# Storing the body's outputs through ScalarE's DMA queue instead of SyncE's, in a fused attention and token-mixing kernel

## The chip, the cores and the metric

The kernel runs on one core of one Trainium2 chip. A core has five engines that run their own instruction streams in order: TensorE (PE; its weight loads are listed apart as PEld), VectorE (DVE), ScalarE (ACT), GpSimd (POOL) and SyncE (SP). An engine's stream may also hold DMA issues: the engine waits for what the transfer needs, hands the transfer over, and goes on. SP computes nothing; its stream here is a queue of DMA issues. The metric is the device time of one execution in microseconds; less is better.

## The reference

Eight batches of 3200 rows go through a gated attention with squared ReLU, and its result through a token-mixing layer:

```python
# attention, per batch: z is 3200x64, u and v are 3200x256
scores = (1/S) * z @ z.T
attn   = maximum(scores, 0) ** 2
x      = u * (attn @ v)
# mixing, per batch
wq, wk = x @ w_q, x @ w_k              # 3200x64 each
W_tok  = (1/8) * wq @ wk.T             # 3200x3200
out    = maximum(W_tok @ x, 0) @ w_out # 3200x256
```

The inputs and the output are float32. The kernel never forms `W_tok`: it computes `wk.T @ x` (64x256, called the heads) and multiplies `wq` by that.

## The kernel before

**Tiling.** The 3200 rows of a batch are 25 tiles of 128. For the output they are taken in 7 groups: six of 512 rows and a last one of 128 (`LASTG`). For each group the program makes the scores of the group against all 25 tiles, squares their ReLU into 16-bit tiles `at`, and multiplies those by `v` in two PSUM accumulators (L289). The scores matrix is symmetric, so a part of the `at` tiles is not computed a second time but turned by a DMA transpose on SP into `tt` and `ttl` (L268) and used in a later group.

**Phases.** The loop from L602 goes through phases k. A phase issues, in this order: six scores matmuls (L211), or four if it also mixes; the ReLU of these on DVE (L234) or ACT (L230); the squares of the scores of the phase before, on POOL (L249) or ACT (L247), with one of ACT's squares sometimes kept back; then the matmuls of the second product (L289), which read `at` tiles of two phases before and turned tiles. After the first ten of these matmuls one extra piece of work may be put in (`extra`, L681 to L701), and behind it stands the square that was kept back (L702). The order of each engine's stream is the order of the program's text.

**What follows a group.** When a group's accumulators are complete, DVE multiplies them by `u` (L315), SP transposes the result to `xT` (L327), and some phases later `keys_and_heads` (L528) makes the projections to queries and keys (L337), ACT copies them (`qk`, L348), SP transposes them to `kx` (L353), POOL doubles a half of `kx` (L362), and TensorE adds the group's share of the heads (L368). When a whole batch's heads are there, its groups are mixed one by one: `mix` (L416), a ReLU on ACT (`rt`, L428), and, as the `extra` of the same phase, `proj` (L441) and `proj_out`, which scales the result by a constant into `fo` and stores it. In the body `proj_out` gets one way: the scaling on ACT (L468), and the store of up to 512 KB on SP (L469). The last group of a batch, with 128 rows, goes a way of its own inside `keys_and_heads`: `side_proj_out` scales on ACT into `fs` (L509) and stores 128 KB on SP (L510). `fo` has two buffers and `fs` one.

**SP's queue.** In the body SP issues, in program order: the loads of `u` (L146), the transposes of `z` (L138), `at` (L268), `xT` (L327) and `kx` (L353), a copy of half of the queries to other partitions (L361), and the stores (L469, L510). An issue that waits holds all those behind it. POOL issues the loads of `v` and `z`.

**Tail.** After the loop (from L716) what is left of the last two batches is mixed and stored by `store`, with queues of its own: SP, and for one store of 256 KB ACT (L751). This is the only DMA that ACT issues.

Of the kernel before, what the change touches and what calls it, by code (L numbers as in the profile page):

```python
# [16 lines left out]
def kernel(  # L17
# [10 lines left out]
    nc = tc.nc  # L28
# [4 lines left out]
    P = 128  # L33
    NT = S // P
    ND = D // P
    W = 512
    widths = [512] * 6 + [128]
# [32 lines left out]
    def ps_tile(name):  # L70
        return pps.tile([P, 2, W], FP32, tag="ps", name=name)
# [9 lines left out]
    def rows(t, b):  # L81
        return t[b].rearrange("(p n) d -> p n d", n=NT)
# [122 lines left out]
    def scores(p0):  # L205
        pair = tiles[p0 : p0 + 2]
        sc = ps_tile("sc")
        for h, (b, gi, ti) in enumerate(pair):
            gs, gw = starts[gi], widths[gi]
            half = h * dqk  # L210
            nc.tensor.matmul(  # L211
                out=sc[:, h, 0:gw],
                lhsT=zT[b][half : half + dqk, ts(ti, P)],
                rhs=zT[b][half : half + dqk, ds(gs, gw)],
                start=True,
                stop=True,
            )
        return sc
# [192 lines left out]
    def mix(b, gi):  # L411
        gw = widths[gi]
        ps = ps_tile("mx")
        for db in range(ND):
            half = db * dh
            nc.tensor.matmul(  # L416
                out=ps[:, db, 0:gw],
                lhsT=hss[b][half : half + dh, ds(db * P, P)],
                rhs=qks[b, gi][half : half + dh, 0:gw],
                start=True,  # L420
                stop=True,
            )
        return ps
# [6 lines left out]
    def proj(b, gi, banks=None):  # L430
        rt = rts.pop((b, gi))
        nj = widths[gi] // P
        ps = None
        if banks is None:
            ps = ps_tile("fo")
            banks = [ps[:, 0, :], ps[:, 1, :]]
        for jf in range(0, nj, 2):
            n = min(2, nj - jf)
            for dc in range(ND):
                for j in range(jf, jf + n):  # L440
                    nc.tensor.matmul(  # L441
                        out=banks[jf // 2][:, ds((j - jf) * D, D)],
                        lhsT=rt[:, dc, ts(j, P)],
                        rhs=wo[:, dc, :],
                        start=(dc == 0 and j == jf),
                        stop=(dc == ND - 1 and j == jf + n - 1),
                    )
        return banks if ps is None else ps[:].rearrange("p a w -> p (a w)")

    def proj_out(b, gi, src, ways):  # L450

        n0 = starts[gi] // P
        if groups:
            fo = pfo.tile([P, 2, W], FP32, tag="fo", name="fo")
        else:
            fo = pg.tile([P, 2, W], FP32, tag="g", name="fo")
        flat_out = fo[:].rearrange("p a w -> p (a w)")
        at = 0
        for on_dve, queue, n in ways:
            sl = slice(at * D, (at + n) * D)  # L460
            part = src[at // 2][:, 0 : n * D] if isinstance(src, list) else src[:, sl]
            if on_dve:
                nc.vector.tensor_scalar(  # L463
                    out=flat_out[:, sl], in0=part, scalar1=FINAL_SCALE, scalar2=None,
                    op0=AOP.mult,
                )
            else:
                nc.scalar.mul(out=flat_out[:, sl], in_=part, mul=FINAL_SCALE)  # L468
            queue.dma_start(  # L469
                out=rows(out, b)[:, n0 + at : n0 + at + n, :],  # L470
                in_=flat_out[:, sl].rearrange("p (n d) -> p n d", d=D),
            )
            at += n
# [33 lines left out]
    def side_proj_out(b, ps):  # L507
        fo = pfo.tile([P, D], FP32, tag="fs", name="fs", bufs=1)
        nc.scalar.mul(out=fo[:], in_=ps[:, 1, D : 2 * D], mul=FINAL_SCALE)  # L509
        nc.sync.dma_start(out=rows(out, b)[:, NT - 1, :], in_=fo[:])  # L510


    todo_mix, todo_between, at_phase, side = [], [], {}, []
# [72 lines left out]
    def mix_due(k):  # L586
        if len(groups) > NG:
            return todo_mix and k - mixed_at[0] >= 3
        older = todo_mix and todo_mix[0][0] < last - 1
        return (older or len(todo_mix) > 2) and k - mixed_at[0] >= 2 and not key_due(k)  # L590
# [11 lines left out]
    while groups:  # L602
        now[0] = k
        for fn in at_phase.pop(k, []):
            fn()
        n = 4 if k == 0 else 6
        mixing = None
        if mix_due(k):
            mb, mg = todo_mix.pop(0)
            mixed_at[0] = k  # L610
            mixing = (mb, mg, mix(mb, mg))
            n = 4
        n = min(n, NTILE - produced)
        fresh = []
        for p0 in range(produced, produced + n, 2):
            fresh.append((p0, scores(p0)))
        produced += n
        made_by.append(produced)
        keying = not mixing and key_due(k)
        if keying and keyed:  # L620
            for g_ in keyed[0][1]:
                double_keys_queries(keyed[0][0], g_)
        if mixing:
            mix_out(*mixing)
        staged = []
        act_pair = 0 if (gate_pending or k < 4) else 1
        for i, (p0, sc) in enumerate(fresh):
            on_act = i == act_pair and not mixing
            staged.append((p0, first_stage(p0, sc, on_act)))
        if k < 3:  # L630
            turn_first(k + 1)
        if k < 2:

            for i, (p0, g) in enumerate(staged):
                second_stage(p0, g, i != 1)
            staged = []
        if len(waiting) == 3:
            second_on_act = [False, True, k % 2 == 0]
        else:
            second_on_act = [False, True]  # L640
        seconds = [(p0, g, a) for (p0, g), a in zip(waiting, second_on_act)]
        acts = [x for x in seconds if x[2]]
        for x in seconds:
            if not x[2]:
                second_stage(*x)
        for x in acts[:1]:
            second_stage(*x)

        if k == 0:
            k += 1  # L650
            continue
        ready = made_by[k - (1 if k < 3 else LAG)]
        b, gi = groups[0]
        begins = left is None
        if begins:
            group_begun(k, b, gi)
            need = ends[b, gi]
            scored = tiles[consumed:need]
            left = [t for t in range(NT) if (b, gi, t) not in scored]
            m = 2 if need <= made_by[k - 1] else 3 if need <= produced else 4  # L660
            if m == 4 and need > produced + (4 if mix_due(k + 1) else 6):
                m = 5
            if gi == LASTG:
                m = 1 if need <= ready else 2
            sizes = [NT * (i + 1) // m - NT * i // m for i in range(m)]
            if k == 1:
                sizes = [2, 4, 4, 5, 5, 5]
        size = sizes.pop(0)
        closes = not sizes
        new = min(ready, ends[b, gi]) - consumed  # L670
        if not closes:
            new = min(new, size)
        rows_ = [t for _, _, t in tiles[consumed : consumed + new]]
        old = len(left) if closes else min(len(left), size - new)
        rows_ += left[:old]
        left = left[old:]
        consumed += new
        assert rows_ and (not closes or consumed == ends[b, gi]), (k, b, gi, sizes)
        gate_pending = False
        matmuls = second_product(b, gi, rows_, begins, closes)  # L680
        extra = None  # L681
        if mixing:
            mb, mg, _ = mixing

            def extra():
                proj_out(mb, mg, proj(mb, mg), [(False, nc.sync, widths[mg] // P)])
        elif keying:
            extra = todo_between.pop(0)[1]
        cut = 10 if extra else 0
        if closes and (b, gi) == (last, LASTG):  # L690
            assert not extra
            cut = 20

            def extra():
                last_gram(last, LASTG - 1, psg)

            psg = acc_tile(1, "xtx")
        for fn in matmuls[:cut]:
            fn()
        if extra:  # L700
            extra()  # L701
        for x in acts[1:]:  # L702
            second_stage(*x)
        for fn in matmuls[cut:]:
            fn()
        if closes:
            group_done(k, b, gi)
            gate_pending = True
            groups.pop(0)
            left = None  # L710
        waiting = staged
        k += 1
# [69 lines left out]
```

## Time and profile before

| | |
|---|---|
| time, median of 3 runs | 803.76 us (801.42 to 806.72) |
| time of the profiled execution | 803.47 us |
| its span, first to last instruction | 801.7 us |
| PE busy | 787.7 us (98%) |
| DVE, ACT, POOL busy | 493.5 us, 476.8 us, 481.6 us |
| SP's hardware queue, share of the 16 DMA engines' span | 76.7% |
| POOL's software queue, the same | 17.8% |
| stores in the body | 40 of `fo`, 7 of `fs` |

Busy time of ACT does not count the issuing of DMAs. A DMA issue on SP has a duration of its own (how long the issue took) and a time to landing (from the issue to the arrival of the last byte): for the stores of 512 KB the median landing is 4.3 us, for `kx` 3.6 us. The matmuls' recorded durations overlap (a matmul of 256 columns has 273 ns, and the next one starts about 109 ns after it), so PE is judged by gaps and waits and not by its busy share.

### The profile page before, as it was taken

What the parts mean: (1) busy time and instruction counts of PE and PEld (TensorE: products, weight loads), DVE (VectorE), ACT (ScalarE), POOL (GpSimd) and SP (SyncE); (2) the same over time, 40 slices, a digit from 0 to 9 for tenths busy, and PEclk for the clock granted to TensorE, in tenths of its full rate; (3) what the DMA queues carried; (4) which work ended last, traced back from release to release, by engine and by line L of the source; (5) the groups of instructions that cost most, each with busy time, mean ns of one, the idle gap of its engine ahead of it and who ended that gap; (6) DMA issues with size and microseconds to landing.
All of it is one profiled execution on the core that took longest, in us unless ns stands there. A gap on an engine that the chain in (4) does not pass through costs nothing.

```text
span 801.7 us, 16689 instructions
## 1 busy us (share of the span) xinstructions
PE 787.7 (98%) x6778; PEld 584.6 (73%) x6778; DVE 493.5 (62%) x514; ACT 476.8 (59%) x528; POOL 481.6 (60%) x350
## 2 busy tenths in 40 slices
PE   7999999999999999999999999999999999999996
PEld 4777777777777777777777777777777767777784
DVE  5766666665665566755667556765666655675535
ACT  6655556556665666655566566656665565586534
POOL 7966677565666557755575556764677646454520
PEclk9999999999999999999999999999999999999999
DMA  7999799997989969999899979999899997769725
GB/s 176 145 215 193 125 175 181 211 192 136 216 144 227 195 137 203 164 213 177 189 160 195 206 176 169 179 184 203 179 179 175 185 204 170 159 147 208 178 50 224
DMA packets 330877, 143.20 MB, mean 179 GB/s; under 512 B 307440, under 2 KB 313136, under 8 KB 330800
## 3 DMA queue, kind: packets, MB, share of 16 engines
q1 hardware_dynamic: 302528, 125.90, 76.7%
q0 software_dynamic: 28128, 15.98, 17.8%
q8 instruction: 53, 0.87, 0.5%
q10 hardware_dynamic: 144, 0.26, 0.1%
q14 instruction: 24, 0.20, 0.1%
HBM read 59.38 MB, written 26.21 MB: 107 GB/s over the span
## 4 chain that ended last, share of the span: by engine, by line
PE 96%; issue 1%; ACT 1%; DVE 1%; POOL 0%; DMA 0%; POOLq 0%; DVEq 0%
PE acc L289 69%; PE sc L211 14%; PE fo L441 5%; PE qk L368 3%; PE qk L337 3%; PE mx L416 2%; PE ztp L118 0%; DMA z<-in_z_dram 0%; ACT g L230 0%; DVE fo L463 0%; POOL at L249 0%; PE qk L499 0%; PE xtx L393 0%; DVE g L234 0%; PE hd L403 0%
## 5 line engine op out<-in xcount | busy, mean ns | idle before, releaser
L249 POOL TENSOR_TENSOR at<-g 128x1024 f16<-128x1024 f32 (+1 forms) x232 | 426.4, 1851 | 231.5 <-DVE g L234 147.4
L234 DVE TENSOR_SCALAR g<-sc 128x1024 f32<-128x1024 f32 (+1 forms) x341 | 389.6, 1185 | 187.8 <-PE sc L211 185.6
L289 PE MATMUL acc<-v_sb,at 128*128 128x256 f16 x3656 | 447.0, 273 | 0.0
L289 PEld LDWEIGHTS <-at 128*128 128x128 f16 x3656 | 344.7, 98 | 107.6 <-issue 64.9
L230 ACT ACTIVATE g<-sc 128x1024 f32<-128x1024 f32 x127 | 130.0, 1024 | 192.9 <-PE sc L211 192.8
L247 ACT ACTIVATE at<-g 128x1024 f16<-128x1024 f32 (+2 forms) x236 | 239.0, 1029 | 0.6 <-DVE g L234 0.6
L289 PE MATMUL acc<-v_sb,tt 128*128 128x256 f16 x1152 | 149.1, 273 | 0.0
L211 PE MATMUL sc<-zT 64*128 64x512 f16 x920 | 129.3, 381 | 1.4 <-ACT zT L122 0.9
L289 PEld LDWEIGHTS <-tt 128*128 128x128 f16 x1152 | 112.5, 98 | 12.9
L315 DVE TENSOR_TENSOR x_sb<-acc,u_sb 128x512 f16<-128x512 f32 (+1 forms) x104 | 69.4, 668 | 64.2 <-PE acc L289 62.8
L428 ACT ACTIVATE rt<-mx 128x1024 f16<-128x1024 f32 (+1 forms) x49 | 49.3, 1010 | 61.7 <-PE mx L416 60.1
L211 PEld LDWEIGHTS <-zT 64*128 64x128 f16 x920 | 34.9, 95 | 48.6 <-issue 26.9
L362 POOL COPY kx<-kx 128x256 f16<-128x256 f16 (+1 forms) x54 | 20.2, 380 | 61.9 <-DMA kx<-qk 59.9
L468 ACT ACTIVATE fo<-fo 128x1024 f32<-128x1024 f32 (+1 forms) x41 | 41.5, 1013 | 23.1 <-PE fo L441 21.2
L441 PE MATMUL fo<-wo,rt 128*128 128x256 f16 x386 | 49.9, 273 | 1.0 <-DVE fo L463 0.9
L348 ACT CAST qk<-qk 128x512 f16<-128x512 f32 (+1 forms) x54 | 28.7, 544 | 25.5 <-PE qk L368 14.5
L441 PEld LDWEIGHTS <-rt 128*128 128x128 f16 x386 | 37.3, 98 | 6.8 <-issue 1.4
L381 DVE TENSOR_TENSOR ha<-ha,qk 128x256 f32<-128x256 f32 x31 | 13.1, 421 | 32.8 <-ACT qk L348 32.8
L337 PE MATMUL qk<-xT_sb,wqk 128*128 128x512 f16 (+1 forms) x108 | 29.9, 358 | 0.0
L368 PE MATMUL qk<-x_sb,kx 128*128 128x256 f16 x191 | 28.4, 273 | 1.4 <-POOL kx L362 1.4
L368 PEld LDWEIGHTS <-kx 128*128 128x128 f16 x195 | 18.9, 98 | 13.7 <-POOL kx L362 2.1
L289 PE MATMUL acc<-v_sb,ttl 128*128 128x256 f16 x192 | 22.6, 273 | 0.0
(47 smaller groups left out, 148.9 us busy)
## 6 DMA issues: line engine op xcount, KB each, us to landing
u_sb<-in_u_dram SPq DMA_DIRECT2D x48, 512.0 KB, 4.7
out_dram<-fo SPq DMA_DIRECT2D x46, 512.0 KB, 4.3
v_sb<-in_v_dram POOLq DMA_DIRECT2D x35, 320.0 KB, 6.0
qk<-qk SPq DMA_DIRECT2D x47, 64.0 KB, 4.0
zd<-in_z_dram POOLq DMA_DIRECT2D x7, 400.0 KB, 7.9
tt<-at SPq DMA_TRANSPOSE x146, 4.4
u_sb<-in_u_dram SPq DMA_DIRECT2D x8, 128.0 KB, 2.9
xT_sb<-x_sb SPq DMA_TRANSPOSE x56, 4.0
```

The lines of the kernel that those rows point to most:

```text
L211: nc.tensor.matmul(out=sc[:, h, 0:gw], lhsT=zT[b][half : half + dqk, ts(ti, P)], rhs=zT[b][half : half + dqk, ds(gs, gw)], start=True, sto ...
L230: nc.scalar.activation(out=g[:, hs, 0:w], in_=sc[:, hs, 0:w], func=RELU, scale=GSCALE)
L234: nc.vector.tensor_scalar(out=g[:, hs, 0:w], in0=sc[:, hs, 0:w], scalar1=0.0, scalar2=GSCALE, op0=AOP.max, op1=AOP.mult,)
L247: nc.scalar.square(out=out, in_=g[:, hs, 0:w])
L249: nc.gpsimd.tensor_mul(out=out, in0=g[:, hs, 0:w], in1=g[:, hs, 0:w])
L289: nc.tensor.matmul(out=accs[j // 2][:, ds((j % 2) * D, D)], lhsT=weights(b, gi, ti, j), rhs=vs[b][:, ti, :], start=(first and ti == rows_[ ...
L315: nc.vector.tensor_mul(out=xs[b, gi][:, 2 * half : 2 * half + n, :].rearrange("p n d -> p (n d)"), in0=accs[half][:, 0 : n * D], in1=us[b, ...
L337: nc.tensor.matmul(out=out, lhsT=w[:, ac, :, :].rearrange("p t h -> p (t h)"), rhs=xTs[b, gi][:, 0 : gw // P, ac, :], start=(start and ac ...
L368: nc.tensor.matmul(out=ps[:, 1, 0:D], lhsT=ks[b, gi][:, n, :, :].rearrange("p a h -> p (a h)"), rhs=xs[b, gi][:, n, :], start=((gi, n) == ...
L428: nc.scalar.activation(out=rts[b, gi][:, :, 0:gw], in_=ps[:, :, 0:gw], func=RELU)
L441: nc.tensor.matmul(out=banks[jf // 2][:, ds((j - jf) * D, D)], lhsT=rt[:, dc, ts(j, P)], rhs=wo[:, dc, :], start=(dc == 0 and j == jf), st ...
L468: nc.scalar.mul(out=flat_out[:, sl], in_=part, mul=FINAL_SCALE)
```

## The change

Two stores change their queue, and nothing else: the one of `fs` in `side_proj_out`, and the one of `fo` that `proj_out` makes when it is called as the `extra` of a mixing phase. The instruction moves from SP's stream to ACT's, right behind the scaling whose result it stores. The tail's stores stay as they are.

```diff
     def side_proj_out(b, ps):
         fo = pfo.tile([P, D], FP32, tag="fs", name="fs", bufs=1)
         nc.scalar.mul(out=fo[:], in_=ps[:, 1, D : 2 * D], mul=FINAL_SCALE)
-        nc.sync.dma_start(out=rows(out, b)[:, NT - 1, :], in_=fo[:])
+        nc.scalar.dma_start(out=rows(out, b)[:, NT - 1, :], in_=fo[:])
...
             def extra():
-                proj_out(mb, mg, proj(mb, mg), [(False, nc.sync, widths[mg] // P)])
+                proj_out(mb, mg, proj(mb, mg), [(False, nc.scalar, widths[mg] // P)])
```

## The prediction

> **What bounds the kernel now.** I read the busy time of each engine by stretches first, because shares over the whole span mix start, body and tail. Columns of the rows: stretch in us, its length, busy us (instructions) of PE, PEld, DVE, ACT and POOL, the granted clock, the DMA engines' share, GB/s.
>
> ```profile
> 20.00:140.00 120.00, 120.00 (x1038) 88.73 (x1036) 76.49 (x79) 70.35 (x78) 88.19 (x64) 1.00 1.05 172
> 140.00:460.00 320.00, 320.00 (x2775) 239.07 (x2772) 200.41 (x208) 193.02 (x214) 195.27 (x136) 1.00 1.00 185
> 460.00:780.00 320.00, 318.61 (x2759) 238.77 (x2757) 194.25 (x204) 191.52 (x212) 183.14 (x130) 1.00 0.90 172
> ```
>
> From 20 to 780 us PE is without work for 1.39 us in all, and the matmuls in it follow each other about every 0.109 us (18 of 256 columns in 1.96 us in the chain of waits), so it isn't a long stall counted as busy. ACT works 60% of the same time. The DMA engines' share is 0.9 to 1.05, which sums packets that may overlap: transfers have little room. The list of waits names PE's idle time; columns: us in total, times, longest.
>
> ```profile
> PE qk L368 <- POOL kx L362: 1.4, 1, 1.4
> PE fo L441 <- DVE fo L463: 0.9, 1, 0.9
> ```
>
> The first is the body's only PE wait. The second lies in the tail at 793.9 us, whose stores the change leaves alone. So a gain in the body can't exceed 1.4 us, 0.17% of 803: the question is whether the change makes PE wait.
>
> **What is removed from SP.** The 47 stores of the body: 40 of fo (L469) and 7 of fs (L510). The rows of these two tiles give durations (ns, min/median/max):
>
> ```profile
> L469 SPq DMA_DIRECT2D out_dram<-fo x50: 327/396/1195, 146.3 to 797.5; - x50
> ...
> L469 ACTq DMA_DIRECT2D out_dram<-fo x1: 374/374/374, 796.8 to 796.8; - x1
> ...
> L510 SPq DMA_DIRECT2D out_dram<-fs x7: 531/538/1146, 176.7 to 749.8; - x7
> ```
>
> Added up one by one, those 47 are 24 us less issuing on SP, which issues for 618 us of the span by the sum of its rows; SP's waits for ACT's scaling in front of a store go too (29.4 us in 9 waits in SP's list). The DMAs behind them on SP, the transposes of at, xT and kx and the loads of u, leave that much earlier. I price this at zero, because what covers it is large: pairing each transposed tile with the first matmul that reads it, in program order, a transpose of at lands at least 10.1 us before its reader. Only kx was once too late (the 1.4 us above). Its store was issued at 654.86, after that kx transpose (648.51), so its removal doesn't help it. Bound of the gain: 0 to 1.4 us; I take 0.
>
> **What is added to ACT.** Per store the issue itself, and a wait for the scaling's own end, where now the next ACTIVATE begins 0.09 us before the scaling ends. The one ACT row (0.37 us) lies in the tail with little beside it; SP's 47 body stores took 0.33 to 0.60 us in nine of ten cases, 1.20 at most. So 0.09 + 0.02 (from the scaling's end to the issue in the tail) + 0.33 to 0.60 gives 0.44 to 0.71 us a store; I take 0.5, nearer to ACT's own row, and 1.33 as the upper end. 47 x 0.5 is 24 us on an engine that has 305 us idle from 20 to 780. Where they fall decides. Queued behind the store are, in time order:
>
> (a) In 23 cases the ReLU of scores (L230), which would have had to wait for PE anyway, 0.94 to 3.95 us, mostly 1.98. The idle time hides 0.5 us wholly, and 1.33 in 17 cases.
>
> (b) In 24 cases a square (L247), delayed by the full 0.5. The tightest is this, first ACT, then PE, then SP, each by its timeline (start, us, what):
>
> ```profile
> 461.18 1.02 ACT L468 ACTIVATE fo<-fo 128x1024 f32<-128x1024 f32 x1 [0.53 <-PE fo L441]
> 462.10 1.05 ACT L247 ACTIVATE at<-g 128x1024 f16<-128x1024 f32 x1
> 464.19 1.02 ACT L230 ACTIVATE g<-sc 128x1024 f32<-128x1024 f32 x1 [1.04 <-PE sc L211]
> ```
>
> ```profile
> 460.98 1.69 PE L289 MATMUL acc<-v_sb,at 128*128 128x256 f16 x14
> 462.51 1.04 PE L289 MATMUL acc<-v_sb,tt 128*128 128x256 f16 x8
> 463.48 0.82 PE L211 MATMUL sc<-zT 64*128 64x512 f16 x6
> 464.23 1.26 PE L289 MATMUL acc<-v_sb,at 128*128 128x256 f16 x10
> ```
>
> ```profile
> 460.57 1.22 SPq L268 DMA_TRANSPOSE ttl<-at  x1
> 461.88 2.11 SPq L353 DMA_TRANSPOSE kx<-qk  x1
> 464.08 1.26 SPq L327 DMA_TRANSPOSE xT_sb<-x_sb  x1
> 465.40 0.57 SPq L146 DMA_DIRECT2D u_sb<-in_u_dram  x1
> 466.07 0.38 SPq L469 DMA_DIRECT2D out_dram<-fo  x1
> ```
>
> The square ends at 463.15; the last two of the ten matmuls from 464.23 read it first, at 465.12: 1.97 us to spare. In the other 23 it is 1.97 to 10.3. The next ReLU follows 1.04 us later here, which absorbs the rest. The SP rows show the other side: this store waits 3.87 us behind three transposes and a load, since the scaling ended at 462.20.
>
> (c) The ReLU of the mix (L428) is needed by PE at once: most have 0.4 us or less before their matmul. It stands two or three phases behind a store, so idle time comes between, except at 657.7 us, where fs, one square and that ReLU follow back to back with 0.06 us to spare.
>
> Following the delay along ACT, less each idle gap, onto squares, ReLUs and the POOL squares that read ACT's g, 0.5 us a store costs PE 0.4 us in all, 0.7 us costs 0.6, 1.33 costs 1.4. The issue term is +0.4 us.
>
> **What is moved in time.** Stores begin 2.5 us earlier in the mean (9.3 at most), in a queue of their own beside SP's. 9 of 54 kx transposes and 13 of 56 of xT then share time with a store that they didn't share with before. The trace has no row for what that costs one of them. From below: nothing, or even a gain, since other stores move away from a transpose. From above: the 4.3 us that a 512 KB store takes to land. The slack of those 9 kx, less 0.45 for POOL's copy, is 0.1, 1.82, 2.07, 2.61, 3.06 and more, of the 13 xT once 0.98: with 1 us each PE loses 0.9, with 2 us 3.1, with 4.3 us about 15 at most. I take 1 us, nearer to the low end since the bytes stay the same, and a kx alone already varies between 2.3 and 8.1 us: +0.9.
>
> The profiled execution took 803.47 us, 801.7 span and 1.8 around it; the median of the runs is 803.76, 0.3 more. 803.47 + 0.4 + 0.9 - 0 = 804.8. What can be told from no change is about 1% here, 8 us: no change.
>
> **The rivals.**
>
> *Starved issue (slower).* An ACT store might not get issued while SP issues transposes, one behind the other. For it: SP issues 77% of the time, and 31 of 47 scalings end inside a transpose's issue. Against it: SP's own stores take 0.6 us or less right behind transposes. Price by the same propagation: if a store waits for the transpose then being issued and two more behind it, it holds ACT 3.2 us in the mean and costs PE 20 us: 803.5 + 20 + 0.9 = 824. With three more it is 4.1 us and 48 us. It decides from a mean hold of about 2.5 us, where the sum passes 8 us.
>
> *Lock on the running transpose (within 1%).* The same wait, for the transpose being issued alone: 1.76 us at most and 1.25 us a store in the mean with the issue, which costs PE 1.6 us in place of 0.4: 806. With one more transpose it is 2.3 us and 5.5 us: 810. For and against it speaks the same.
>
> The Trainium skill, Perfetto Trace Analysis, section "DMA Instruction — HWDGE (DVE, Sync)", speaks against the change here: the block that generates descriptors is locked for one sequencer while it generates, and the wait for that lock is inside the DMA instruction's recorded time. By that rule the lock case holds in place of the forecast; no run here shows two sequencers at it in the body.
>
> *Crowded transposes (slower).* The store in a second queue takes the DMA engines from kx and xT for its whole landing time: +15 + 0.4, 819. For it: a DMA share of 0.9 to 1.05, and the kx that PE waited for was 6.7 us in flight. Against it: one queue carried the same bytes.
>
> *SP relieved (faster).* At most 1.4 us by the rows, 802; more than 1% would need a PE wait that the trace doesn't hold.
>
> *It does nothing.* If ACT's issue is as hidden as its idle time and the transposes don't notice: 803.5.
>
> **How the numbers follow.** Forecast, with the case that nothing shows, 0.66; lock 0.12; starved 0.12; crowded 0.07; faster by over 1%, 0.03 (runs that differ from the profiled one). Within 1%: 0.66 + 0.12 = 0.78; slower by over 1%: 0.19; faster 0.03. The runs spread from 801.4 to 806.7, 2.3 below to 2.9 above their median. Low: 803.5 - 1.4 - 2.1 = 800. High: the lock's 810 and most of the way to the crowded case, 816; left out are the starved case and the rest, about 0.17.
>
> **What would show it.** Right: PE's waits in 20 to 780 us stay below 4 us; the store on ACT takes 0.3 to 0.6 us, and the idle time before L230 shrinks by about it; SP loses 47 issues and its wait for ACT's fo. Starved: ACT stores of 2 us and more, and PE waits for ACT's at or rt. Crowded: PE or POOL waits for kx or xT grow, with landings above 3.6 and 4.0 us. I'm wrong if a body transfer that PE needs at once hung on a store's place in SP's queue, or if ACT's row in the tail says nothing of the body.

## The result and the profile after

| | before | after |
|---|---|---|
| median | 803.47 us (6 runs, 801.42 to 809.10) | 813.55 us (6 runs, 809.62 to 816.31) |
| profiled execution / its span | 803.47 / 801.7 us | 814.76 / 813.0 us |
| mean granted clock in it | 0.999 | 0.992 |

The ratio is 1.0107, with a 95% interval of 1.0080 to 1.0134: slower by about 1%, or 10 us. First the same stretches of the changed kernel (stretch, its length, busy us of PE, PEld, DVE, ACT and POOL, granted clock, DMA share, GB/s):

```profile
20.00:140.00 120.00, 120.00 (x1038) 88.85 (x1036) 76.48 (x80) 70.35 (x78) 87.65 (x64) 1.00 1.08 172
140.00:460.00 320.00, 315.24 (x2719) 234.98 (x2719) 194.79 (x204) 189.85 (x210) 193.53 (x135) 0.99 0.99 182
460.00:780.00 320.00, 316.19 (x2709) 234.25 (x2709) 196.41 (x204) 193.86 (x213) 182.68 (x128) 0.99 0.92 174
```

Nothing happens up to 140 us, before the first store of the body. After that PE lacks work for 4.8 and 3.8 us, where it lacked 0 and 1.4, and the granted clock isn't full any more. PE's list of waits says for whom (us in total, times, longest):

```profile
PE qk L368 <- POOL kx L362: 3.8, 1, 3.8
...
PE sc L211 <- ACT g L230: 3.1, 1, 3.1
PE sc L211 <- ACT rs L491: 1.7, 1, 1.7
```

The two waits for ACT are new. They stand at 262 and 264 us, and ACT's timeline shows why. First the place in the kernel before, where ACT goes on to its next ReLU and waits for PE there:

```profile
251.26 1.02 ACT L468 ACTIVATE fo<-fo 128x1024 f32<-128x1024 f32 x1 [0.53 <-PE fo L441]
254.27 1.02 ACT L230 ACTIVATE g<-sc 128x1024 f32<-128x1024 f32 x1 [1.98 <-PE sc L211]
```

Then the same place in the changed kernel:

```profile
250.93 1.02 ACT L468 ACTIVATE fo<-fo 128x1024 f32<-128x1024 f32 x1 [0.50 <-PE fo L441]
260.69 0.34 ACTq L469 DMA_DIRECT2D out_dram<-fo  x1
261.07 1.02 ACT L230 ACTIVATE g<-sc 128x1024 f32<-128x1024 f32 x1 [9.12 <-DMA tt<-at]
```

The scaling of batch 1, group 1, ends at 251.95, and its store is issued at 260.69. ACT does nothing for 9.1 us, and the release is given as a DMA that has nothing to do with the store: a transpose of `at` to `tt`. The chain of waits of the changed kernel, in order of time (start, us, what), passes through the same place:

```profile
252.00 0.58 SPq L268
...
252.67 7.94 DMA tt<-at
...
260.63 0.02 ACTq L469
...
260.69 0.34 ACTq L469
```

SP issues the transpose at 252.67; it lands at 260.61; 0.02 us later an instruction of 17 ns on ACT, of the store's line, has what it waited for, and the store goes. That instruction is in the rows of the store's line (duration in ns, min/median/max):

```profile
L469 ACTq DMA_DIRECT2D out_dram<-fo x41: 338/339/376, 142.1 to 808.1; - x41
L469 ACTq EVENT_SEMAPHORE  x40: 17/17/17, 141.0 to 764.6; - x40
```

The semaphore events of the trace tell the rest. A completion semaphore is a counter that a transfer raises when its data has landed. In these kernels the transfers of SP and ACT have eight of them between them, handed out in turn, and an issue waits until the transfer that had the same semaphore before has landed. In the kernel before that is the eighth transfer back in SP's order in 475 of 477 cases, in the changed kernel the sixth to eleventh back in the program's order. The store that was ready at 251.95 shares its semaphore with a transpose six transfers back. SP's timeline:

```profile
242.15 5.16 SPq L268 DMA_TRANSPOSE tt<-at  x2
247.41 3.80 SPq L138 DMA_TRANSPOSE zT<-zd  x1
251.31 2.77 SPq L268 DMA_TRANSPOSE tt<-at  x2
```

SP was late, held up behind a transpose of `z` (247.41 to 251.21), and hadn't even issued the transpose in question, the second of the last row, when the store was ready.

So the store left SP's stream, but not SP's backlog: ACT, with computing to do, now waits for it. Six of the 47 stores were held for over 0.3 us in this execution, 13.2 us together; one of the holds, 8.7 us, is longer than the slack behind it.

The lost clock is the second part. Two stretches of the body ran at half clock: 264.0 to 267.4, from the end of the second wait for ACT on, and 663.4 to 670.2, which begins within the wait for kx (660.5 to 664.2). Both, and the stretch behind the first:

```profile
264.00:267.40 3.40, 2.96 (x14) 1.80 (x14) 3.40 (x4) 2.24 (x3) 1.89 (x1) 0.50 1.14 250
267.40:270.80 3.40, 3.40 (x31) 2.41 (x30) 0.36 (x2) 0.62 (x1) 0.00 (x0) 1.00 0.71 138
663.40:670.20 6.80, 5.97 (x28) 3.27 (x29) 0.94 (x2) 2.97 (x5) 5.95 (x4) 0.50 0.94 205
```

In 3.4 us 14 matmuls ran at half clock and 31 behind it at the full one. PE worked for 3.0 and 6.0 us in the two stretches at half clock, so by estimate they cost half of that, about 4.5 us. Together: PE's waits grew from 1.4 to 8.6 us (+7.2), and +4.5 for the clock, 11.7 in all; the spans differ by 11.3. Of the 11.7 some 6.3 stand at the hold of ACT near 260 us, and some 5.4 at the wait for kx, at which ACT was held for no more than 0.8 us.

The other theories that this leaves are that the stores, earlier and in a queue of their own, crowd the transposes of kx (the wait at 664 us grew from 1.4 to 3.8 us, and has the longer stretch at half clock behind it), and that 47 issues on ACT simply cost too much.

### The profile page after: what moved, and what is told of

It is laid out like the page before. It is cut to its first block, busy times and chain, and to the rows that moved or that the text cites. A ratio compares the mean times of both kernels' runs of the same rounds, so it can differ in the third digit from the quotient of the medians.

```text
span 813.0 us, 16641 instructions
## 1 busy us (share of the span) xinstructions
PE 791.9 (97%) x6778; PEld 586.3 (72%) x6778; DVE 492.1 (61%) x514; ACT 478.1 (59%) x528; POOL 481.5 (59%) x350
## 4 chain that ended last, share of the span: by engine, by line
PE 94%; issue 2%; DMA 1%; ACT 1%; DVE 1%; POOL 1%; SPq 0%; ACTq 0%; POOLq 0%; DVEq 0%
PE acc L289 68%; PE sc L211 14%; PE fo L441 5%; PE qk L368 3%; PE qk L337 2%; PE mx L416 2%; DMA tt<-at 1%; POOL at L249 0%; ACT g L230 0%; PE ztp L118 0%; DVE g L234 0%; DMA z<-in_z_dram 0%; DVE fo L463 0%; ACT at L247 0%; PE qk L499 0%
## 5 line engine op out<-in xcount | busy, mean ns | idle before, releaser
L289 PE MATMUL acc<-v_sb,ttl 128*128 128x256 f16 x192 | 22.6, 273 | 0.0
```

The lines of the kernel that those rows point to most:

```text
L289: nc.tensor.matmul(out=accs[j // 2][:, ds((j % 2) * D, D)], lhsT=weights(b, gi, ti, j), rhs=vs[b][:, ti, :], start=(first and ti == rows_[ ...
```

## The experiments

Each ratio is against runs of the kernel before on the same chip, with its 95% interval.

**One store back on SP**, that of batch 1, group 1:

```diff
-                proj_out(mb, mg, proj(mb, mg), [(False, nc.scalar, widths[mg] // P)])
+                queue = nc.sync if (mb, mg) == (1, 1) else nc.scalar
+                proj_out(mb, mg, proj(mb, mg), [(False, queue, widths[mg] // P)])
```

> One store of the 47, that of batch 1, group 1, goes back to SP; the other 46 stay on ACT. Theory 1 (the store waits on ACT for the landing of an earlier transfer that uses the same completion semaphore): ACT's 9.1 us of idle time behind that scaling disappears, with PE's two waits there (3.1 + 1.7 us) and the half clock of 3.4 us behind them, which cost about 1.5 us: some 6 us less than the changed kernel, about 807. Theory 2 (stores in their own queue crowd the kx transposes): no change, about 813, since the kx wait at 664 us is untouched. Theory 3 (47 issues on ACT): no change, 813.

Measured: 810.13 us, 1.0093 (1.0063 to 1.0122). PE's waits near 260 us are gone in the profile, and its longest wait for kx was 2.5 us, with 3.4 us of half clock. The time hardly fell, though: by 3.4 us between the medians, by 1.1 going by the ratios. Theory 1's 807 lies below the interval, whose lower end is 808.6 us (1.0063 x 803.49, the median before on that chip); the 813 of theories 2 and 3 lies inside it. So the time speaks against a loss of 6 us by this one hold in the changed kernel. Once more:

> The store of batch 1, group 1, back on SP, once more, for a second profile of what remains: theory 1 expects the remaining 5 to 7 us over the kernel before in holds of ACT in front of the stores of batches 2 to 5, with lengths that change from run to run; theory 2 expects it in the wait for kx near 660 us and the half clock behind it.

808.86 us, 1.0076 (1.0046 to 1.0107). The profile shows ACT held for 2.5 us at 447 us and 0.9 at 544, with no PE wait from it, and again a kx wait (2.1 us) with 3.4 us of half clock behind it: in this profile the answer of theory 2. Both profiles were taken in executions near the lower end of their kernel's runs (807.08 of 807.08 to 814.24; 805.9 of 805.12 to 816.12), so what the longer ones lost isn't in them. One profile is one draw of something that varies.

**The other suspect back on SP**: the same edit with `(5, 1)`, the store ahead of the long kx wait.

> One store of the 47, that of batch 5, group 1, goes back to SP; the other 46 stay on ACT. Theory 2: PE's wait for kx near 664 us falls from 3.8 us to the 1.4 of the kernel before, and the half clock behind it (6.8 us, about 3.0 lost) goes: some 5 us less than the changed kernel, about 808. Theories 1 and 3: the wait for kx stays near 3.8 us and the time near 813.

808.22 us, 1.0071 (1.0043 to 1.0099; 11 runs from 804.85 to 815.05). That is the answer of theory 2, in the time (808) and in the profile, where PE doesn't wait for kx near 660 us at all. It doesn't decide, though. The interval overlaps that of the changed kernel, the profile is of the fastest of the 11 runs, and in it the hold of batch 1, group 1, which this edit doesn't touch, was 1.7 us in place of 8.7: the holds vary by execution.

**That one store alone on ACT**, the other 46 on SP:

```diff
-                proj_out(mb, mg, proj(mb, mg), [(False, nc.sync, widths[mg] // P)])
+                queue = nc.scalar if (mb, mg) == (1, 1) else nc.sync
+                proj_out(mb, mg, proj(mb, mg), [(False, queue, widths[mg] // P)])
```

> The kernel before, with one store alone on ACT, that of batch 1, group 1. Theory 1: this one store holds ACT for 8 to 9 us, PE waits 4 to 5 us and runs at half clock for 3 to 4 us behind it: 6 us over the kernel before, about 809.5. Theories 2 and 3: one store can't cost more than some tenths: 803.5.

809.46 us, 1.0065 (1.0040 to 1.0089): a single store costs some 5 us in the mean. Its 12 runs lie between 803.91 and 813.43; the profile is of the fastest of them, with a hold of 2.2 us that cost nothing, so a costly one is not on record for this kernel. Neither crowding by 47 stores nor 47 issues can explain its time.

**The hold without the store.** All stores on SP, and ACT kept busy behind the same scaling:

```diff
                 nc.scalar.mul(out=flat_out[:, sl], in_=part, mul=FINAL_SCALE)
+                if groups and (b, gi) == (1, 1):
+                    for _ in range(10):
+                        nc.scalar.copy(out=spare[:], in_=flat_out[:, sl])
```

> The kernel before, all stores on SP, with ten copies of 128x1024 on ACT into a spare tile behind the scaling of batch 1, group 1, which keep ACT from its next ReLU for about 9.3 us. If the hold of ACT is what costs, whatever holds it (theory 1): PE waits 4 to 5 us near 260 us, half clock behind it, 6 us over the kernel before, about 809.5. If the store's transfer itself is at fault (theory 2): 803.5 to 804.

811.35 us, 1.0120 (1.0087 to 1.0153), somewhat more than the 6 us expected; the ten copies held ACT for 10.7 us, where 9.3 were expected. PE's list of waits of this kernel:

```profile
PE sc L211 <- ACT g L230: 4.6, 1, 4.6
...
PE sc L211 <- ACT rs L496: 1.3, 1, 1.3
```

They are the two waits of the changed kernel, 5.9 in place of 4.8 us, with 6.8 us of half clock, which began within the first. Holding ACT at this place costs PE its time without any store on ACT.

**The bare issue.** All stores on SP, and a copy of about an issue's length behind each scaling on ACT:

```diff
                 nc.scalar.mul(out=flat_out[:, sl], in_=part, mul=FINAL_SCALE)
+                if groups:
+                    nc.scalar.copy(out=spare[:, 0:448], in_=flat_out[:, 0:448])
...
         nc.scalar.mul(out=fo[:], in_=ps[:, 1, D : 2 * D], mul=FINAL_SCALE)
+        nc.scalar.copy(out=spare[:, 0:D], in_=fo[:])
+        nc.scalar.copy(out=spare[:, 0:D], in_=fo[:])
```

> The kernel before, all stores on SP, with a copy on ACT into a spare tile behind each of the body's 47 scalings (128x448 behind fo, two of 128x256 behind fs), which takes as long as the issue of a store on ACT. Theory 3: if the bare issue time on ACT is what costs, most of the 10 us come back: 811 to 814. Theories 1 and 2: 0.4 us by the prediction's propagation, 803.5 to 804.5.

804.43 us, 0.9997 (0.9980 to 1.0013). The group of these copies in this kernel (busy us, mean ns, idle time before):

```profile
L472 ACT COPY spare<-fo 128x448 f32<-128x448 f32 x40 | 22.6, 564 | 1.3
```

28 us of work more on ACT, these 22.6 and 5.6 behind fs, cost nothing that can be measured: the slack that the prediction counted is there, and theory 3 is out.

**The stores through POOL**, as early as on ACT, and in a queue with semaphores of its own (`nc.gpsimd` in place of `nc.scalar` in both lines of the change):

> The 47 stores go through POOL's queue, which issues transfers with semaphores of its own, in place of ACT's. Theory 1: ACT doesn't wait for stores any more, PE's wait near 260 us is gone; what comes in its place is an issue of about 0.6 us on POOL, whose squares have 1.25 us to spare at least, and POOL's own wait for the scaling: 803.5 to 807. Theory 2: stores are as early as on ACT and crowd kx just as much, so PE waits for kx of 2 us and more remain: 808 or more.

804.36 us, 1.0011 (0.9981 to 1.0040). POOL's list of waits of this kernel:

```profile
POOL out_dram L469 <- ACT fo L468: 141.1, 39, 6.3
```

POOL stands for 141 us in front of its stores, which go out 0.30 us behind their scaling in the mean (0.31 on ACT), and the time is that of the kernel before. PE's only wait in the body is for kx, in this profile with 3.4 us of half clock:

```profile
PE qk L368 <- POOL kx L362: 4.1, 1, 4.1
```

So stores that leave early and outside SP's queue cost at most 0.4%; the rest of the loss takes the holds of ACT. POOL's transfers are in another queue than ACT's, so this bounds crowding by ACT's queue only by analogy; the next run bounds it directly.

**The stores of group 1 of every batch**, put back on SP (`nc.sync if mg == 1 else nc.scalar`, 7 of 47), and, the other way round, alone on ACT:

> The stores of group 1 of every batch (7 of the 40 fo stores, issued on ACT a few us after SP has the transpose of the next z in front of its queue) go back to SP; 33 fo and 7 fs stores stay on ACT. Theory 1 (a store on ACT waits until an earlier transfer with the same completion semaphore has landed, and that one is stuck in SP's queue behind z): ACT's waits in front of stores fall from 14 us to under 5, and the time to 804 to 806. Theory 2 (40 stores in their own queue crowd the kx transposes): nothing of it goes, except where one of the seven was next to a kx; 808 or more. Theory 3 (the issues): 40 of 47 remain, 812.

> The counterpart of the run that put group 1's stores back: these 7 stores alone on ACT, the other 40 on SP. Theory 1 (the wait for an earlier transfer in SP's queue): nearly the whole loss with a sixth of the stores, 809 to 813, and ACT held for 2 to 9 us in front of one or more of them. Theory 2 (crowding) and theory 3 (issues): 7 of 47, at most 2 us, 804 to 806.

Put back: 806.13 us, 1.0017 (0.9990 to 1.0043). Alone on ACT: 810.08 us, 1.0077 (1.0047 to 1.0107). Seven stores carry most of the loss, and the other forty, still on ACT, none that can be measured, 0.43% at most. The profile of the first is of an execution of 813.76 us, against the median of 806.13. ACT's holds in it come to 5.7 us, one of them 5.1 at batch 2, group 0, which cost PE nothing. PE's longest wait is one of 6.5 us for kx with 6.8 us of half clock, although the store of group 1 next to it is on SP there. So a long kx wait isn't tied to that store; forty others are on ACT in this kernel. The profile of the second, of an execution of 804.94 us, has holds of 1.7 and 2.3 us that cost nothing.

**The changed kernel again:**

> The changed kernel once more, beside the others on one chip. Theory 1: the waits of ACT in front of a store are long again at the stores of group 1 (250, 450, 550 or 650 us), with lengths that differ from those of the first profile since they depend on how far SP is behind: ACT's sum 5 to 20 us, time 810 to 816. Theory 2: the wait for kx near 660 us is the part that recurs.

811.54 us, 1.0096 (1.0059 to 1.0134). ACT was held for 6.8 us at batch 1, group 1, 5.0 at batch 2, group 0, 1.7 at batch 3, group 1; PE waited 1.1 and 1.7 us near 261 us, and 2.8 us for kx in two waits, the longer, 2.0, near 660 us, all without a stretch of half clock in the body. The profile is of an execution near the lower end (808.92 us; the six lie between 808.57 and 818.18). The hold at batch 1, group 1, recurs, its length changes; the wait for kx recurs too.

**Moving z.** The transposes of `z`, but the first, two phases later, with the stores on ACT and with the stores on SP:

```diff
-            due(k + later + 10, lambda: turn_z(b + 1))
+            due(k + later + (10 if b == 0 else 12), lambda: turn_z(b + 1))
```

> The changed kernel with the transposes of z, but the first, issued two phases (some 7 us) later, so that they leave SP behind the point at which group 1's scaling ends and not ahead of it. Theory 1: the transfer that group 1's store must wait for is no longer behind z, so its wait falls below 2 us, unless another store now falls into the stretch behind z; within 0.5% of the next kernel. If the wait comes from the queues in general and not from z's burst: ACT is held as long as before, 810 to 814.

> The kernel before with the same shift of z's transposes, for comparison: theory 1 lets it be what it was, 803 to 805, since SP's stores hold nobody; the wait for kx near 655 us, which lay behind such a transpose, may go (1.4 us) or move.

With the stores on ACT 814.95 us, 1.0145 (1.0101 to 1.0189); with the stores on SP 803.53 us, 1.0002 (0.9985 to 1.0019). The 0.5% was missed: the gap between the two is larger than before. The other answer, ACT held as long as before, is nearer: 19.1 us in this profile, against 13.2. The profile is of an execution of 820.53 us (the six lie between 810.60 and 821.95), and names the exception that was left open, in ACT's timeline:

```profile
663.72 0.38 ACT L509 ACTIVATE fs<-qk 128x256 f32<-128x256 f32 x1 [0.49 <-DVE ha L381]
673.09 0.38 ACTq L510 DMA_DIRECT2D out_dram<-fs  x1
673.51 1.06 ACT L247 ACTIVATE at<-g 128x1024 f16<-128x1024 f32 x1 [9.41 <-DMA tt<-at]
674.48 1.01 ACT L428 ACTIVATE rt<-mx 128x1024 f16<-128x1024 f32 x1
```

The hold at batch 1, group 1, shrank to 0.8 us as expected. But now the store of fs at 664.1 met SP's backlog (the transpose of `z` took 9.3 us to issue, from 653.73), was held for 9.0 us, and the ReLU that PE needs at once stood two places behind it: PE waited 9.4 us. So the burst of `z` moved, and a hold with it. But `z` isn't the only backlog: the store of batch 2, group 0, was held for 5.5 us until a copy of queries (L361) had landed, which SP, busy with transposes of `at` and `xT`, had issued 1.1 us after the store was ready; it was held there for 5.0 and 5.1 us in two profiles in which `z` wasn't moved.

**What the profiles say together.** In the nine profiles of kernels with body stores on ACT there are 30 holds of over 0.3 us. In every one the store's semaphore is the one that the issue waits for, and the store goes 0.08 us after the last increment of it by the transfer that had it before. That is theory 1's mechanism. Theory 2 is not dead, though. In the eight profiles with forty or more stores off SP, PE's longest wait for kx was 3.8, 2.0, 2.5, 2.1, 1.0, 4.1, 6.5 and 4.5 us, six times with a stretch of half clock; in the six with at most seven stores off SP it was 1.4, 2.1, 1.5, 1.6, 1.7 and none, once with one. Stores outside SP's queue may lengthen these waits. What that costs in the mean is bounded by the runs through POOL and with group 1 put back, 0.4% each, and may be nothing.

## Why the prediction was right and wrong

The range, 800 to 816, held the median of 813.55 by luck: its upper end was made from the lock and from crowding, and the holds that made most of the loss were in neither. The forecast of no change was missed narrowly: the best estimate is 1.07%, with an interval across the bound of 1%. By its own sign it failed: PE's waits in 20 to 780 us were to stay below 4 us, and came to 8.6. The time of 804.8 was 8.7 us short, above all by one step, the wait on ACT.

- **What bounds the kernel, and the ceiling of the gain.** Right. SP lost its 47 issues and waits longer in front of the transposes of `at` instead (141 us before and 179 after, for POOL's and ACT's squares and ACT's g); nothing came of the relief.
- **The issue on ACT.** Right in size: 0.338 to 0.376 us a store against 0.33 to 0.60 assumed, and the copies show that such an amount is hidden.
- **"Per store the issue itself, and a wait for the scaling's own end".** This is the step that failed: there is a third part, the wait for the transfer that had the completion semaphore before. There was a sign of it. The rows of the store's line in the kernel before have semaphore instructions under the row that the prediction quoted; for what they wait, the row doesn't say, but the semaphore events of the same trace do:

```profile
L469 SPq EVENT_SEMAPHORE  x46: 17/17/17, 146.3 to 797.1; - x46
```

On SP this wait never showed as a cost: SP's list of waits in the kernel before has none of L469 for a DMA. The stream there is in the order in which transfers get their semaphores, so by the time the store is at its head, the transfer eight places back has mostly landed; and whoever waits on SP keeps no engine from computing. Moved to ACT, the store is ready while SP still has that transfer ahead of it. Where the term had 0.4 us, one store alone on ACT cost 0.65% (5 us) and the seven of group 1 alone 0.77% (6 us). The term's upper end of 1.33 us doesn't come out of its parts (0.09 + 0.02 + 1.20 is 1.31); nothing hangs on that.
- **The price of a wait.** The prediction took each wait of PE at its own length. The half clock that came with the waits, 4.5 of the 11.7 us in the first profile after, was in no term.
- **Starved issue.** Right in kind (an ACT store stuck behind SP's transposes), wrong in mechanism and count: not every store behind whatever SP issues, but a few, each behind one certain earlier transfer (six of 47 over 0.3 us).
- **Lock on the running transpose.** Wrong. 30 of the 47 ACT stores were issued while SP was inside the issue of a transpose, and these took 0.338 to 0.376 us like the rest. The rule of the Trainium skill, Perfetto Trace Analysis, section "DMA Instruction — HWDGE (DVE, Sync)", that the descriptor generator is locked for one sequencer, shows no wait here.
- **Crowded transposes.** The 0.9 us taken for it lies within what the run through POOL leaves (between -0.2% and +0.4%). The 15 us of the rival does not. The longer kx waits of the profiles with many stores off SP leave open whether something of it is real.

Still open is how the loss is shared among the seven stores of group 1, and how much of it is the waits for kx. The one of batch 1 alone costs 0.65%, but without it 0.76 to 0.93% remain, so the parts don't add up, and no profile caught an execution that shows a long hold at another of them in the changed kernel without it. Costly holds are on record in the two profiles of the changed kernel, in that with `z` moved and, with copies in place of the store, in the run that kept ACT busy; the profiles of the runs with one store and with seven alone are of executions of 803.91 and 804.94 us, which show no loss. A store on ACT with a semaphore that no transfer of SP uses wasn't tried; the run through POOL stands in for it.

## What to carry to other kernels

In a kernel built like this one a DMA issue carries a wait for whoever had its completion semaphore before, and in the engine that issues it everything behind waits along: read the semaphore instructions in front of an issue before moving it to an engine that computes. Moving a store out of a congested queue doesn't separate it from that queue if both draw on the same semaphores; look where the queue is furthest behind, and ask which engine can afford to stand still there. Where a stall depends on a backlog, run several executions before believing one profile's list of waits.

## What the runs showed of the hardware

A wait of PE of a few us costs more than itself. With waits of 2.1, 2.5, 4.1 and 4.5 us came 3.4 us at half clock, with 3.8, 4.6 and 6.5 us 6.8, with 9.4 us 10.2: whole multiples of 3.4 us. Two waits of 3.1 and 1.7 us close together brought 3.4 as well. The half clock doesn't begin where the wait ends. With the wait of 2.1 us it began 1.4 us after the end, with that of 4.6 us 3.1 us after the beginning, with that of 9.4 us 2.0 us after the beginning. What it costs is half of the time that PE works in it: by estimate 1.7 us where a stretch of 3.4 lies wholly behind the wait, and 1.4 of the 10.2, of which PE worked for 2.8. With single waits of 1.4 to 1.7 us the clock stayed full, as it did once with 2.0 and once with 1.1 and 1.7 close together. The Trainium skill, TensorE: Matmul & The Clock Gate, section "Part 1: The HAM clock gate", has half rate after an idle window of some 3.4 us; the steps of 3.4 us agree, but here waits shorter than that were enough.
